# GpSimd's additions, subtractions and x's transposes moved behind another VectorE operation in a fused convolution and feed-forward kernel

## The chip, the cores and the metric

The kernel runs on one core of a Trainium2 chip. The metric is the device time of one execution in microseconds (us), the median over several runs. TensorE (PE in the profile; PEld is its weight load) does matrix products, VectorE (DVE), ScalarE (ACT) and GpSimd (POOL) do elementwise work, and SyncE (SP) issues most transfers. Each engine works through its own instructions in order.

## The reference

A light convolution over time (seven taps, one weight set for each of 8 heads) is followed by a feed-forward layer without gating, whose activation is a smooth step between -1 and 1:

```python
x_unf = x_pad[:, idx, :].reshape(B, S, K, H, group)      # B, S, D = 8, 4096, 192; K = 7, H = 8
x = np.einsum('hk,bskhg->bshg', softmax(weight), x_unf).reshape(B * S, D)
h = x @ w_in                                              # 192 x 2048
g = np.where(h >= 1, h, np.where(h <= -1, 0.0, (h + 1) ** 2 / 4))
return g @ w_out                                          # 2048 x 192
```

## The kernel before

**Tiles and steps.** The 32768 tokens are cut into 64 tiles of 512. A tile has 8 steps, one for each 256 of the 2048 hidden units, so there are 512 steps q. Tiles go in pairs c of 16 steps, called a period here; i is the step's number in its period, tile 2c has i from 0 to 7 and tile 2c+1 has i from 8 to 15. After the first 16 steps every product of 32-bit numbers is made of three products of a high half (rounded by ScalarE's copy to the matmul's 32-bit format) and a low half (what the rounding left, by a subtraction).

**One step** is written down in the main loop in this order: `mm1(q)` (18 matmuls on each half of the array, into one of two PSUM tiles `h`), `mm2(q - 3)`, `act_both(q)` (ScalarE: Relu and Square), on some steps `evac_banks` (four copies by ScalarE), `act_low(q - 2)` (VectorE: the low half of the activation, 128x1024, from two operands in SBUF), the slot of the convolution, `act_sum(q - 2)` (VectorE: the sum of two low halves), transfers and transposes of the output, `act_hi(q - 1)` (ScalarE) and `act_most(q)` (VectorE: reads `h` in PSUM and thereby frees it for `mm1(q + 2)`). `mm1` reads the tile's inputs in the order n, s, r: as they are, swapped between the partitions' halves, and the last 64 channels. In each of n and s it takes two matmul pairs on the high half and then one on the low half, so the swapped low half (`"s", "lo"`) comes with the second pair of low matmuls of the step.

**The convolution** for the tiles to come is spread over the steps in three units of a pair c: `a` is the first 128 channels of tile 2c, `b` those of tile 2c+1, `r` the last 64 channels of both. A unit is transposed by VectorE (`"T"`), gets its seven taps (0 to 6), and is split into a high and a low half, each of which is copied into a swapped version by two transfers on SP's queue (`swapped`). The plans say which step does what: `PLAN_A` and `PLAN_R` and the first part of `PLAN_B` (i of 12 and more) run in the period before the pair's own, the rest of `PLAN_B` (i under 8) in the pair's own first tile. `conv_slot` carries a plan out. Unit a's taps are VectorE's; a tap of b or r is a product on ScalarE (`product`) and an addition on GpSimd.

**Order of GpSimd's additions.** From c = 2 on, `taps` puts an addition into the list `held`. `add_held` issues the list behind the slot and makes each addition wait for that step's `act_sum`, so that it doesn't run beside `act_low`:

```python
add_held(act_sum(n) if low else None)
```

The subtraction that makes a low half in `split` for a and b is issued in the slot itself and waits for nothing but its operands. `evac_add` issues accumulating transfers on GpSimd's queue in the fourth and fifth step of each tile.

Of the kernel before, what the change touches and what calls it, by code (L numbers as in the profile page):

```python
# [8 lines left out]
F32 = mybir.dt.float32  # L9
# [22 lines left out]
def lightconv_then_ffn(ctx: ExitStack, tc: tile.TileContext, x, weight, w_in, w_out, out):  # L32
# [24 lines left out]
    nc = tc.nc  # L57
# [53 lines left out]
    def load_unit(c, u, engs=None):  # L111
        ta, tb = 2 * c * TB, (2 * c + 1) * TB
        if u == "rb":
            return load_raw([tb, tb, tb + TB // 2, tb + TB // 2], [P, P + SQ, P, P + SQ], engs,
                            TB // 2)
        if u == "r":
            return load_raw([ta, ta, tb, tb], [P, P + SQ, P, P + SQ], engs)
        return load_raw([ta if u == "a" else tb] * 4, [0, SQ, 2 * SQ, 3 * SQ], engs)
# [2 lines left out]

    pending = []

    held = []

    def add_held(behind):

        for out, a, b in held:
            add = nc.gpsimd.tensor_add(out, a, b)  # L129
            if behind is not None:  # L130
                tc.add_manual_dep(add.ins, behind.ins.name, mybir.DependencyInfo(
                    mybir.DependencyClass.Sync, mybir.DependencyReason.DATA), reason="port")
        held.clear()

    def let_go():

# [10 lines left out]
    class Conv:  # L147
# [92 lines left out]
        def taps(self, *ks):  # L240
            y = self.y
            for k in ks:
                if k == 0:
                    nc.scalar.mul(y, self.xT[:, SH:SH + TB], wk[:, self.wsel, 0:1])  # L244
                elif self.c == 1 and self.u != "b":
                    pending.append((y, y, self.product(k)))
                elif self.c > 1:
                    held.append((y, y, self.product(k)))
                else:
                    nc.gpsimd.tensor_add(y, y, self.product(k))  # L250

# [4 lines left out]
            nc.sync.dma_start(out=w[BOT].bitcast(F32), in_=t[TOP].bitcast(F32))  # L256
            return w

        def split(self, eng=None):
            for _ in self.splits(eng or nc.gpsimd):  # L260
                pass

        def splits(self, eng):

            o = xop[2 * self.c + (self.u == "b")]
            hi = xo.tile([P, TB], F32R, name="hi0")
            lo = xo.tile([P, TB], F32R, name="lo0")
            nc.scalar.copy(hi, self.y)
            for key, t in (("hi", hi), ("lo", lo)):
                if key == "lo":  # L270
                    yield
                    eng.tensor_sub(lo, self.y, hi.bitcast(F32))
                w = self.swapped(t, key + "1", 3)
                o["n", key] = (t[TOP], t[BOT])
                o["s", key] = (w[TOP], w[BOT])
            yield

        def split_rest(self):

# [157 lines left out]
    NQ = NSB * NPAIR  # L437
# [63 lines left out]
    turns = tc.alloc_semaphore("turns")  # L501
# [79 lines left out]
    def act_sum(q):  # L581
        gt = stage.tile([P, CC], F32R, name="m")[:, 0:TB]
        gts[q] = gt
        gl = gls[q].bitcast(F32)
        return nc.vector.tensor_add(gt, gl[:, 0, :], gl[:, 1, :])  # L585
# [214 lines left out]
    def whole(j, *cols):  # L800
        for _ in chunks[j].bits(*cols):
# [19 lines left out]
    conv_b, conv_rb = Conv(0, "b", raw_b), Conv(0, "rb", raw_rb)  # L821
# [5 lines left out]

    PLAN_B = {12: ("T",), 14: (0, 1), 15: (2, 3), 1: (4,), 2: (5,), 3: (6,), 5: "split"}  # L830
    PLAN_A = {1: ("T",), 2: (0,), 4: (1,), 6: (2,), 7: (3,), 9: (4,), 10: (5,), 11: (6,),
              12: "split"}
    PLAN_R = {2: ("T",), 4: (0,), 6: (1,), 7: (2,), 8: (3, 4), 9: (5,), 11: (6,), 13: "split"}
    SECOND_B = {0: (0, 1), 1: (2,), 2: (3,), 3: (4,), 4: (5, 6), 5: "split"}


# [2 lines left out]
    FIRST_A = {7: ("T", 0, 1, 2), 8: (3, 4), 9: (5, 6), 11: "split"}  # L839
    FIRST_R = {8: ("T",), 9: (0,), 10: (1, 2), 11: (3, 4), 12: (5, 6), 13: "split"}  # L840

    def conv_slot(i, b, a, r):
        early = b is not None and b.c == 0
        plans = ((None if early else b, SECOND_B if b and b.c == 1 else PLAN_B),
                 (a, FIRST_A if early else PLAN_A),
                 (r, FIRST_R if early else PLAN_R))
        for u, plan in plans:
            what = plan.get(i, ()) if u else ()
            if what == "split":
                if u is r:  # L850
                    u.split_rest()
                else:
                    u.split()
                continue
            if "T" in what:
                u.transpose()
            ks = [k for k in what if k != "T"]
            if ks:
                (u.taps_dve if u is a and not early else u.taps)(*ks)

# [5 lines left out]
    def parts_hi(q):  # L868
        for n, rest in PARTS.get(q, ()):
            chunks[n].hi(rest)  # L870
# [95 lines left out]
    conv_n, ahead = {}, {}  # L966
    for q in range(NQ + LATE):
        s, j = divmod(q, NPAIR)
        c, i = divmod(q, 2 * NPAIR)
        if q < NQ and i == 0 and c > 0:  # L970
            conv_b = conv_n["b"]
        if q < NQ and i == (0 if c > 0 else 4):
            conv_n, ahead = ahead, {}
            if c > 0 and c + 1 < NB:
                for u in "arb":
                    if u not in conv_n:
                        conv_n[u] = Conv(c + 1, u, load_unit(c + 1, u))
        if c == 0 and i in (4, 5, 10):
            u = {4: "a", 5: "r", 10: "b"}[i]
            conv_n[u] = Conv(1, u, load_unit(1, u))  # L980
        if i == (14 if c == 0 else 8) and c + 2 < NB:
            ahead = {u: Conv(c + 2, u, load_unit(c + 2, u)) for u in "ar"}

        done = q - (DELAY if q < NF32 + DELAY else LATE)
        if done < 0 or q == NF32 + DELAY:
            done = None
        if q == NPAIR:
            mm2_first(done)
        if q < NQ:
            mm1(q)  # L990
        if done is not None and q != NPAIR:
            (pair_last if done == NQ - 1 else mm2 if done >= NF32 else mm2_first)(done)

        if q < 2:
            (step_0, step_1)[q]()
        elif q < NPAIR:
            first_step(q)
        elif q < NF32:
            if q == NPAIR + 1:
                evac(0)  # L1000
            if q == 2 * NPAIR - 2:
                pending.extend(late)
            let_go()
            act_clip(q)
            act_square(q)
            parts_hi(q + 1)
            parts_lo(q, (True,))
            let_go()
            act_max(q)
            parts_lo(q, (False,))  # L1010
            conv_slot(i, conv_b, conv_n.get("a"), conv_n.get("r"))
            if j >= NPAIR - 2:
                store(0, "mr"[j - NPAIR + 2])
        else:
            if q == NQ - 1:
                act_hi(q - 1)
            if q < NQ:
                act_both(q)
            if done is not None and done % NPAIR == NPAIR - 1 and done < NQ - 1:
                (evac if done < NF32 else evac_banks)(done // NPAIR)  # L1020
            if done == NQ - 2:
                evac_last(done // NPAIR)
            if q == NF32:
                parts_lo(q)
            n = q - 1 if q < NF32 + 3 else q - 2
            low = n in ghs and n not in gls
            ahead_of = q in (NF32 + 2, NF32 + 3)
            if low:
                act_low(n)
            if ahead_of:  # L1030
                act_most(q)
            if q < NQ:
                conv_slot(i, conv_b if i < 8 else conv_n.get("b"), conv_n.get("a"),
                          conv_n.get("r"))
            add_held(act_sum(n) if low else None)
            if q == NQ - 1:
                act_low(q - 1)
                act_most(q)
                act_sum(q - 1)
            if q < NQ:  # L1040
                if s > 2 and j in (3, 4):
                    evac_add(s - 1, j - 3)
                if s <= 2 or s == NSB - 1:
                    m = 6 if s > 2 else 2
                    if m <= j < m + 2:
                        store(s - 1, "mr"[j - m])
                elif j == NPAIR - 1:
                    store(s - 1, "m")
                if j == 0 and s > 3:
                    store(s - 2, "r")  # L1050
            if q - 1 in gs and q - 1 not in ghs and q < NQ:
                act_hi(q - 1)
            if q < NQ - 1 and not ahead_of:
                act_most(q)
            if q < NF32 + 2:
                act_hi(q)
        if i == 2 * NPAIR - 1 and c == 0:
            conv_n["b"].transpose()
        if q == NQ - 4:
            plain = ob.tile([P, TB // SQ, SQ], F32, name="osb").rearrange("p j b -> p (j b)")[:, 0:P]  # L1060
            diagonal(plain, 0)
# [26 lines left out]
```

## Time and profile before

| | |
|---|---|
| median of 3 runs | 2046.57 us (2046.46 to 2049.79) |
| the profiled execution: time, span of its instructions | 2046.76 us, 2045.0 us |
| PE busy | 2037.9 us (100%) |
| PEld busy | 1756.9 us (86%) |
| DVE busy | 1966.2 us (96%) |
| ACT busy | 1960.4 us (96%) |
| POOL busy | 792.8 us (39%) |

Busy time is the union of an engine's instructions over the span. The ends of matmuls are modelled, and neighbours on an engine overlap a little, so a share near 100% doesn't tell whether an engine ever waits. The chain of work that ended last lies to 68% on PE, 15% on DVE and 13% on ACT. L579 is `act_low`, L585 `act_sum`, L890 `act_most`, L562 and L563 `act_both`, L573 `act_hi`, L475 `mm1`, L528 `mm2`, L129 the additions of `add_held`, L272 the subtraction of `splits`, L255 and L256 the swap copies, L163 the units' transposes, L631 the output's, L232 VectorE's taps, L237 ScalarE's products.

### The profile page before, as it was taken

To read this page: it belongs to the slowest core of one execution; us is meant where nothing else is said; L and a number is where in the kernel's file an instruction comes from. 1 tells how busy PE (TensorE), PEld (TensorE's weight loads), DVE (VectorE), ACT (ScalarE), POOL (GpSimd) and SP (SyncE) were. 2 spreads that over 40 slices of the span, in tenths; PEclk is the share of its full clock that TensorE was granted. 3 is DMA by queue.
4 is the path that set the end of the run, shared out by engine and by line. 5 is a ranking of instruction groups with operands and counts; after the bars stand their busy time and mean duration, and the time that the engine had idled before them with its cause. 6 is when DMAs were issued, how large, how long until landed. Compare 5 with 4: busy or idle time off the path is not lost.

```text
span 2045.0 us, 46902 instructions
## 1 busy us (share of the span) xinstructions
PE 2037.9 (100%) x18644; PEld 1756.9 (86%) x18644; DVE 1966.2 (96%) x2109; ACT 1960.4 (96%) x2381; POOL 792.8 (39%) x749
## 2 busy tenths in 40 slices
PE   9999999999999999999999999999999999999999
PEld 6998888888888888888888888888888888888888
DVE  8899999999999999999999999999999999999998
ACT  8799999999999999999999999999999999999997
POOL 1544343343433443334434344343343333443431
PEclk9999999999999999999999999999999999999999
DMA  7333333443434434334333344343343433433323
GB/s 178 80 62 70 69 71 71 85 76 56 81 68 79 80 65 77 71 67 87 70 66 73 72 82 76 57 83 69 74 81 65 76 71 66 86 72 65 72 55 55
DMA packets 470685, 152.27 MB, mean 74 GB/s; under 512 B 418944, under 2 KB 426624, under 8 KB 470464
## 3 DMA queue, kind: packets, MB, share of 16 engines
q1 hardware_dynamic: 446880, 109.17, 25.4%
q0 software_dynamic: 23424, 39.99, 13.4%
q8 instruction: 146, 2.39, 0.5%
q14 instruction: 75, 0.61, 0.1%
q10 hardware_dynamic: 160, 0.10, 0.0%
HBM read 32.84 MB, written 25.17 MB: 28 GB/s over the span
## 4 chain that ended last, share of the span: by engine, by line
PE 68%; DVE 15%; ACT 13%; issue 4%; DVEq 0%; ACTq 0%; POOL 0%; POOLq 0%
PE h L475 35%; PE accr L528 20%; PE accm L528 10%; DVE gl L579 7%; DVE g L890 4%; ACT gh L573 3%; ACT g L562 3%; ACT g L563 3%; DVE m L585 3%; ACT p L237 3%; DVE osb L631 1%; PE accm L495 1%; PE accr L495 1%; ACT t L609 0%; ACT y L244 0%
## 5 line engine op out<-in xcount | busy, mean ns | idle before, releaser
L579 DVE TENSOR_TENSOR gl<-g,gh 128x1024 fp32r<-128x1024 f32 x495 | 728.1, 1471 | 23.4 <-ACT gh L573 17.1
L890 DVE SCALAR_TENSOR_TENSOR g<-g,h 128x1024 f32<-128x1024 f32 x504 | 607.5, 1206 | 4.8 <-ACT g L563 2.8
L475 PE MATMUL h<-hi,w 64*128 64x512 f32 x4032 | 609.4, 380 | 1.5
L528 PE MATMUL accr<-gh,wg 64*128 64x512 f32 x3960 | 590.1, 376 | 0.0
L562 ACT ACTIVATE g<-h 128x1024 f32<-128x1024 f32 (+1 forms) x497 | 507.2, 1020 | 41.6 <-PE h L475 39.9
L563 ACT ACTIVATE g<-g 128x1024 f32<-128x1024 f32 (+1 forms) x497 | 526.6, 1060 | 15.8
L573 ACT CAST gh<-g 128x1024 fp32r<-128x1024 f32 x495 | 514.4, 1039 | 0.5 <-DVE g L890 0.4
L129 POOL TENSOR_TENSOR y<-y,p 128x512 f32<-128x512 f32 x180 | 231.0, 1283 | 573.3 <-ACT p L237 300.5
L475 PEld LDWEIGHTS h<-hi,w 64*128 64x128 f32 x4032 | 376.0, 186 | 76.4 <-DVE g L890 28.2
L528 PEld LDWEIGHTS accr<-gh,wg 64*128 64x128 f32 x3960 | 373.9, 185 | 53.2
L129 POOL TENSOR_TENSOR r<-r,p 128x512 f32<-128x512 f32 x180 | 232.5, 1291 | 476.6 <-DVE m L585 420.0
L475 PE MATMUL h<-lo,w 64*128 64x512 f32 x2016 | 383.8, 376 | 0.0
L528 PE MATMUL accr<-gl,words 64*128 64x512 f32 x1980 | 376.3, 376 | 0.0
L585 DVE TENSOR_TENSOR m<-gl 128x512 fp32r<-128x512 f32 x495 | 348.0, 703 | 20.6 <-PE h L475 0.5
L528 PE MATMUL accm<-gh,wg 64*128 64x512 f32 x1980 | 295.1, 376 | 0.0
L475 PE MATMUL h<-rh,w 64*128 64x512 f32 x992 | 293.6, 376 | 0.0
L475 PE MATMUL h<-rhi,w 64*128 64x512 f32 x992 | 293.6, 376 | 0.0
L619 POOL DMA_DIRECT2D t<-t x244 | 206.0, 983 | 97.6 <-DMA t<-t 75.6
L475 PEld LDWEIGHTS h<-lo,w 64*128 64x128 f32 x2016 | 192.2, 186 | 25.9
L528 PEld LDWEIGHTS accr<-gl,words 64*128 64x128 f32 x1980 | 188.3, 186 | 26.0
L528 PEld LDWEIGHTS accm<-gh,wg 64*128 64x128 f32 x1980 | 188.0, 186 | 26.0
L475 PEld LDWEIGHTS h<-rhi,w 64*128 64x128 f32 x992 | 184.5, 186 | 12.9
(161 smaller groups left out, 2313.3 us busy)
## 6 DMA issues: line engine op xcount, KB each, us to landing
t<-t POOLq DMA_DIRECT2D x183, 128.0 KB, 4.1
out_dram<-osb SPq DMA_DIRECT2D x366, 64.0 KB, 1.9
raw<-in_x_dram SPq DMA_DIRECT2D x334, 68.0 KB, 2.6
hi<-hi SPq DMA_DIRECT2D x128, 128.0 KB, 3.4
lo<-lo SPq DMA_DIRECT2D x126, 128.0 KB, 3.1
t<-t POOLq DMA_DIRECT2D x61, 256.0 KB, 3.3
rhi<-rh SPq DMA_DIRECT2D x62, 128.0 KB, 4.1
rlo<-rl SPq DMA_DIRECT2D x62, 128.0 KB, 3.5
```

The lines of the kernel that those rows point to most:

```text
L129: add = nc.gpsimd.tensor_add(out, a, b)
L237: nc.scalar.mul(p, self.xT[:, SH + k:SH + k + TB], wk[:, self.wsel, k:k + 1])
L475: nc.tensor.matmul(h[e], w[HALVES[e], c0:c0 + P], seen(x[e][e]), start=(n == 0), stop=(n == len(mms) - 1))
L495: nc.tensor.matmul(accs[s][a, i][:, c0:c0 + D], block, w[half, e, :], start=(j == 0 and e == 0 and b % 2 == 0), stop=(j == NPAIR - 1 and e ...
L528: mm = nc.tensor.matmul(accs[s][bank], w[half], in_turn(g[half]), start=(j == 0 and bank not in seen), stop=(j == NPAIR - 1 and k % 3 == 2 ...
L562: nc.scalar.activation(g[:, e, :], hs[q][:, e, :], AF.Relu, bias=0.5, scale=0.5)
L563: nc.scalar.activation(g[:, e, :], g[:, e, :], AF.Square)
L573: nc.scalar.copy(gh[:, e, :], gs[q][:, e, :])
L579: nc.vector.tensor_sub(gl[:, e, :], g[:, e, :], gh[:, e, :])
L585: return nc.vector.tensor_add(gt, gl[:, 0, :], gl[:, 1, :])
L619: nc.gpsimd.dma_start(out=to, in_=src, accum_op=ALU.add)
L890: nc.vector.scalar_tensor_tensor(out=g, in0=g, scalar=1.0, in1=h, op0=ALU.min, op1=ALU.max)
```

## The change

- `held` gets a second list, `fresh`. What a slot puts into `fresh` is issued by `add_held` one step later, behind that step's `act_sum`. The product on ScalarE is made in the slot as before.
- For a and b of c = 2 and more, the subtraction of the low half (and with it the two transfers of the swapped low half, which are written down behind it) goes into `fresh` as well. The high half and its transfers stay in the slot.
- `conv_slot` is called twice, once ahead of `act_sum` for what is not a transpose and once behind `add_held` for the entries with `"T"`.
- Taps 5 and 6 of r are done by VectorE (`taps_dve`).
- The plans of b, a and r are laid anew; the steps of the three splits stay.

```diff
 
     pending = []
-    held = []
+    held, fresh = [], []
     def add_held(behind):
-        for out, a, b in held:
-            add = nc.gpsimd.tensor_add(out, a, b)
+        for work in held:
+            done = work()
             if behind is not None:
-                tc.add_manual_dep(add.ins, behind.ins.name, mybir.DependencyInfo(
+                tc.add_manual_dep(done.ins, behind.ins.name, mybir.DependencyInfo(
                     mybir.DependencyClass.Sync, mybir.DependencyReason.DATA), reason="port")
-        held.clear()
+        held[:] = fresh
+        fresh.clear()
     def let_go():
...
                 elif self.c == 1 and self.u != "b":
                     pending.append((y, y, self.product(k)))
                 elif self.c > 1:
-                    held.append((y, y, self.product(k)))
+                    fresh.append(lambda p=self.product(k): nc.gpsimd.tensor_add(y, y, p))
                 else:
                     nc.gpsimd.tensor_add(y, y, self.product(k))
...
             nc.sync.dma_start(out=w[BOT].bitcast(F32), in_=t[TOP].bitcast(F32))
             return w
-        def split(self, eng=None):
-            for _ in self.splits(eng or nc.gpsimd):
-                pass
+        def split(self):
+
+            if self.c < 2:
+                for _ in self.splits(nc.gpsimd):
+                    pass
+                return
+            parts = self.splits(nc.gpsimd)
+            next(parts)
+            fresh.append(lambda: next(parts))
         def splits(self, eng):
...
             hi = xo.tile([P, TB], F32R, name="hi0")
             lo = xo.tile([P, TB], F32R, name="lo0")
             nc.scalar.copy(hi, self.y)
+            sub = None
             for key, t in (("hi", hi), ("lo", lo)):
                 if key == "lo":
                     yield
-                    eng.tensor_sub(lo, self.y, hi.bitcast(F32))
+                    sub = eng.tensor_sub(lo, self.y, hi.bitcast(F32))
                 w = self.swapped(t, key + "1", 3)
                 o["n", key] = (t[TOP], t[BOT])
                 o["s", key] = (w[TOP], w[BOT])
-            yield
+            yield sub
         def split_rest(self):
...
-    PLAN_B = {12: ("T",), 14: (0, 1), 15: (2, 3), 1: (4,), 2: (5,), 3: (6,), 5: "split"}
-    PLAN_A = {1: ("T",), 2: (0,), 4: (1,), 6: (2,), 7: (3,), 9: (4,), 10: (5,), 11: (6,),
+    PLAN_B = {13: ("T",), 14: (0, 1), 15: (2,), 0: (3,), 1: (4,), 2: (5,), 3: (6,), 5: "split"}
+    PLAN_A = {1: ("T",), 2: (0,), 4: (1,), 5: (2,), 6: (3,), 7: (4,), 9: (5,), 10: (6,),
               12: "split"}
-    PLAN_R = {2: ("T",), 4: (0,), 6: (1,), 7: (2,), 8: (3, 4), 9: (5,), 11: (6,), 13: "split"}
+    PLAN_R = {3: ("T",), 4: (0,), 6: (1,), 7: (2,), 8: (3,), 9: (4,), 11: (5,), 12: (6,),
+              13: "split"}
     SECOND_B = {0: (0, 1), 1: (2,), 2: (3,), 3: (4,), 4: (5, 6), 5: "split"}
...
     FIRST_A = {7: ("T", 0, 1, 2), 8: (3, 4), 9: (5, 6), 11: "split"}
     FIRST_R = {8: ("T",), 9: (0,), 10: (1, 2), 11: (3, 4), 12: (5, 6), 13: "split"}
-    def conv_slot(i, b, a, r):
+    def conv_slot(i, b, a, r, turns=None):
         early = b is not None and b.c == 0
         plans = ((None if early else b, SECOND_B if b and b.c == 1 else PLAN_B),
                  (a, FIRST_A if early else PLAN_A),
                  (r, FIRST_R if early else PLAN_R))
         for u, plan in plans:
             what = plan.get(i, ()) if u else ()
+            if turns is not None and turns != ("T" in what):
+                continue
             if what == "split":
                 if u is r:
                     u.split_rest()
...
                 u.transpose()
             ks = [k for k in what if k != "T"]
             if ks:
-                (u.taps_dve if u is a and not early else u.taps)(*ks)
+                dve = not early and (u is a or u is r and ks[0] > 4)
+                (u.taps_dve if dve else u.taps)(*ks)
...
             if ahead_of:
                 act_most(q)
             if q < NQ:
-                conv_slot(i, conv_b if i < 8 else conv_n.get("b"), conv_n.get("a"),
-                          conv_n.get("r"))
+                units = conv_b if i < 8 else conv_n.get("b"), conv_n.get("a"), conv_n.get("r")
+                conv_slot(i, *units, turns=False)
             add_held(act_sum(n) if low else None)
+            if q < NQ:
+                conv_slot(i, *units, turns=True)
             if q == NQ - 1:
                 act_low(q - 1)
                 act_most(q)
```

## Rows read from the trace of the kernel before

**Rows 1.** Busy times in windows, 146.65 to 1971.32: busy (instructions) of each engine.

```profile
146.65:1971.32 1824.67, 1821.91 (x16708) 1571.00 (x16705) 1773.50 (x1828) 1774.47 (x2118) 722.32 (x659) 1.00 0.39 73
```

**Rows 2.** Timeline, PE: start us, us, engine, line, operation, operands, count.

```profile
146.65 0.60 PE L475 MATMUL h<-hi,w 64*128 64x512 f32 x4
...
979.91 0.59 PE L475 MATMUL h<-hi,w 64*128 64x512 f32 x4
...
995.45 0.59 PE L475 MATMUL h<-hi,w 64*128 64x512 f32 x4
...
1971.32 0.59 PE L475 MATMUL h<-hi,w 64*128 64x512 f32 x4
```

**Rows 3.** Table of waits: who waited for whom, total us, times, longest us.

```profile
PEld h L475 <- DVE g L890: 28.2, 83, 0.5
```

**Rows 4.** Groups of instructions: busy us, mean ns, idle before and its releasers.

```profile
L579 DVE TENSOR_TENSOR gl<-g,gh 128x1024 fp32r<-128x1024 f32 x495 | 728.1, 1471 | 23.4 <-ACT gh L573 17.1
...
L237 ACT ACTIVATE p<-r,wk 128x512 f32<-128x512 f32 x180 | 124.1, 705 | 0.0
...
L232 DVE SCALAR_TENSOR_TENSOR y<-xT,wk,y 128x512 f32<-128x512 f32 x186 | 138.6, 745 | 0.1
...
L163 DVE STREAM_TRANSPOSE r<-raw 128x544 f32<-128x544 f32 x30 | 22.0, 732 | 0.0
```

**Rows 5.** Timeline, POOL and DVE, 965 to 967.5.

```profile
965.46 2.65 POOL L129 TENSOR_TENSOR y<-y,p 128x512 f32<-128x512 f32 x2 [2.33 <-ACT p L237]
...
966.91 2.28 DVE L579 TENSOR_TENSOR gl<-g,gh 128x1024 fp32r<-128x1024 f32 x1 [0.17 <-ACT gh L573]
```

**Rows 6.** Timeline, POOL and SP, around one split of b.

```profile
989.61 1.27 POOL L272 TENSOR_TENSOR lo<-y,hi 128x512 fp32r<-128x512 f32 x1 [0.56 <-ACT hi L268]
...
993.38 1.28 POOL L129 TENSOR_TENSOR r<-r,p 128x512 f32<-128x512 f32 x1 [2.49 <-DVE m L585]
...
991.05 1.22 SPq L255 DMA_DIRECT2D lo<-lo  x1
...
992.32 0.60 SPq L256 DMA_DIRECT2D lo<-lo  x1
```

**Rows 7.** Timeline, DVE, steps 3 to 7 of the same period.

```profile
979.92 1.53 DVE L579 TENSOR_TENSOR gl<-g,gh 128x1024 fp32r<-128x1024 f32 x1 [0.28 <-ACT gh L573]
...
983.49 1.53 DVE L579 TENSOR_TENSOR gl<-g,gh 128x1024 fp32r<-128x1024 f32 x1
...
987.34 1.21 DVE L579 TENSOR_TENSOR gl<-g,gh 128x1024 fp32r<-128x1024 f32 x1
...
990.50 1.46 DVE L579 TENSOR_TENSOR gl<-g,gh 128x1024 fp32r<-128x1024 f32 x1
...
992.55 0.68 DVE L585 TENSOR_TENSOR m<-gl 128x512 fp32r<-128x512 f32 x1
...
994.28 1.46 DVE L579 TENSOR_TENSOR gl<-g,gh 128x1024 fp32r<-128x1024 f32 x1
```

**Rows 8.** Timeline, DVE in step 13, and PE two steps later.

```profile
1019.94 0.69 DVE L283 TENSOR_TENSOR rl<-r,rh 128x512 fp32r<-128x512 f32 x1 [0.73 <-ACT rh L282]
1020.55 0.69 DVE L585 TENSOR_TENSOR m<-gl 128x512 fp32r<-128x512 f32 x1
1021.15 1.22 DVE L890 SCALAR_TENSOR_TENSOR g<-g,h 128x1024 f32<-128x1024 f32 x1
...
1022.66 0.60 PE L475 MATMUL h<-hi,w 64*128 64x512 f32 x4
```

**Rows 9.** Line 631 alone: duration min/median/max ns, first and last start, forms.

```profile
L631 DVE STREAM_TRANSPOSE osb<-t x122: 696/708/711, 147.8 to 2036.4; 128x512 f32<-128x512 f32 x61, 64x512 f32<-64x512 f32 x61
```

**Rows 10.** Timeline, PE: second pair of low matmuls in step 8.

```profile
996.53 0.38 PE L475 MATMUL h<-lo,w 64*128 64x512 f32 x2
```

**Rows 11.** Tile lo: its transfers on SP's queue (ns), and DMA to landing.

```profile
L255 SPq DMA_DIRECT2D lo<-lo x63: 461/500/1817, 45.8 to 1997.6; - x63
...
DMA to landing us min/median/max: 2.2/3.1/4.2
```

## What the change is expected to do

> **What bounds the kernel now.** I read the busy times of the steady stretch first [rows 1]: TensorE (1821.91 of 1824.67 us), VectorE (1773.50) and ScalarE (1774.47) are all nearly full, so shares decide nothing. The next question is what a step costs TensorE when nothing holds it, read from its timeline at the first matmul of a step. From the start of one period's step 4, 979.91, to that of its step 8, 995.45 [rows 2], it takes 15.54 / 4 = 3.885 us a step, or 62.16 a period of 16 steps. Over the 29 periods from 146.65 to 1971.32 [rows 2] a period takes 1824.67 / 29 = 62.92. So steady state holds only 0.76 us of waiting a period, some 23 us over the 30 periods that carry the planned work: that is all that the change can win there, whatever it frees on the other engines. The table of waits puts TensorE's loss at weight loads that wait for `act_most` (28.2 us, [rows 3]; a load waits a little earlier than its matmul, so this is the larger figure). The clock was granted in full all the way [rows 1] and plays no part.
>
> Behind `act_most` stands VectorE. `act_low` takes 1.47 us on average [rows 4]. It grows when a GpSimd add runs into it; the worst case is two adds in a row at the end of a period (2.65 us from 965.46), which stretch the next `act_low` to 2.28 [rows 5].
>
> **The change part by part.**
>
> **Adds a step behind.** The product is there a step early, so GpSimd can start right behind `act_sum`, as it does now in step 6, where it waited for nothing else: the sum starts at 992.55 and ends some 0.68 later, the add starts at 993.38, 0.15 after that, and takes 1.28 [rows 6, 7]. `act_most`, which reads one operand from PSUM and follows the sum, covers most of it; what sticks out costs the next `act_low` 0.25 (1.46 at 994.28 against 1.21 at 987.34, [rows 7]). With one add a step the 1.07 of the double add goes (2.28 less 1.21), and so does 0.32 each at 979.92 and 983.49 [rows 7], where the add came late behind its product.
>
> **Transposes behind the sum.** A transpose of 0.73 [rows 4] delays its follower by some 0.66, as neighbours on VectorE overlap by about 0.07 (1019.94 + 0.69 against 1020.55, [rows 8]). Three of them go between sum and `act_most`. The output's transposes stand there already, beside a running add, and keep 0.70 to 0.71 in all 122 cases [rows 9], so I cost the move at no contention, and the transpose completes the add's cover. The price is that `act_most` of that step comes 0.66 later. In steps 1 and 3 VectorE has room. In step 13 it has not: there the low half of r has waited 0.73 for ScalarE's copy, `act_most` ends at 1021.15 + 1.22 = 1022.37, and TensorE takes the freed bank at 1022.66 [rows 8]. B's transpose moves into this step: 1022.37 + 0.66 = 1023.03, 0.37 late. If ScalarE, a product lighter at step 11, reaches r's copy earlier, it is as little as nothing. I take 0.15 a period, nearer to the lower end, since that copy waits for ScalarE alone.
>
> **Two taps to VectorE.** ScalarE loses two products of 0.7, VectorE gains two operations of 0.74 [rows 4], 0.66 in a row. Of VectorE's busy time 1.47 - 1.21 = 0.26 of each `act_low` is blocking, 4.2 a period, of which five cases of 0.25 to 0.28 remain (the adds of steps without a transpose): its demand changes by 1.3 + 1.4 - 4.2 = -1.5. Neither engine becomes the bound in total. By these three parts alone the 0.76 goes, except for the 0.15 of step 13.
>
> **The low halves a step behind.** This part decides, I think. The plan keeps B's split at step 5, and tile 2c+1 starts at step 8 as before. Now GpSimd computes the low half as soon as the high half exists, from 989.61 to 990.88, ahead of step 6's sum, and SP's queue issues the two swap copies at 991.05 and 992.32 [rows 6]. A copy lands 3.1 us after its issue (2.2 to 4.2, [rows 11]), here at 995.4. TensorE begins step 8 at 995.45 [rows 2] and reads the swapped low half in the step's second pair of low matmuls, at 996.53 [rows 10]. The margin is 1.1 us.
>
> Afterwards the subtraction waits for step 6's `act_sum`: it stands where r's add of that step stands, 993.38 to 994.66 [rows 6]. The second copy is issued some 0.6 later (the first holds the queue 0.50, [rows 11]) and lands, at the median, at 994.66 + 0.6 + 3.1 = 998.36, which is 1.83 behind 996.53. VectorE also comes to that sum later. Between step 3's `act_low` and step 6's sum, the late adds take 0.32 twice less, r's transpose comes in with 0.66, an add now stands behind step 4's sum (0.25), A's tap now falls into step 5 (at most 0.66, some 0.5 with the pause that a sum directly behind `act_low` has now), and step 6 loses its own 0.25: +0.5 in all, some 0.1 less since the start of the period is no longer late. That makes 2.2. Against it, the copies now run behind the high halves' copies and the accumulating transfers and no longer among them, so for the landing I take 2.9, below the median of all: **2.0 us a period**. Bounds: 0.9 with the shortest landing and VectorE where it is now, 3.4 with the longest and VectorE 0.5 later. TensorE works in order, so nothing covers the wait; `mm2`'s matmuls stand behind it. Behind the waiting subtraction GpSimd has the next add alone, and behind the copies SP has output stores and loads, which nobody waits for yet.
>
> A's subtraction moves from step 12 to step 13, but its tile starts only at step 16. The sum of step 13 ends at 1020.55 + 0.69 = 1021.24 [rows 8]; with 0.15, 1.28, 0.6 and 2.9 the copy lands at 1026.2. Step 16 starts a step behind 1022.66, at 1026.5, and reads it 1.08 later (as 996.53 less 995.45): 1.4 us in hand, and 0.1 with the longest landing.
>
> The Trainium skill ("SBUF — State Buffer", section "The DMA setup-cost knee") gives a transfer a fixed part of some 2 us plus its bytes at 436 GB/s, for these 128 KB an estimate of 2.3 us. The rows show 3.1 at the median, and they decide; by the page's figure the wait would be 1.4 and the time about 2071.
>
> **The sum.** The profiled execution took 2046.76 us (span 2045.0), 0.2 above the median of the runs. A period changes by +2.0 (swapped low half) + 0.15 (step 13) - 0.76 (the waits of now) = +1.39. B's split stands behind the sum in 30 periods (c from 2 to 31): +41.7, so 2046.8 + 41.7 = **2088.5 us**.
>
> **The rivals.**
> - *Short landing.* Without other transfers beside them the copies land near their shortest, 2.2: the wait is about 1.2 and the time 2046.8 + 30 x (1.2 + 0.15 - 0.76) = 2064.5. For it: now they share the queues with much. Against: 3.1 is the median over all copies, A's too. Chance 0.12. The page named above leans this way.
> - *The swap comes in time, and only the gains count* (faster). The place is step 8's second low pair. It decides if both copies land within 1.3 us of the subtraction's end, with the 0.6 for issuing in it; the shortest landing seen is 2.2 from issue. Or the subtraction isn't held as I read the diff. Then 2046.8 + 30 x (0.15 - 0.76) = 2028.5. Chance 0.05.
> - *VectorE late on top.* The taps and the transposes ahead of `act_most` make step 13 late by the full 0.37, the low half comes at 2.2, and A's swap is late by up to 0.5 too: 2046.8 + 30 x (2.2 + 0.37 + 0.5 - 0.76) = 2116. For it: VectorE hardly idles now. Against: a wait of 2 us at step 8 gives VectorE and ScalarE that much free time in each period. Chance 0.08.
> - My forecast, 2075 to 2105: 0.73. The last 0.02 is a wait so small (near 0.6) that loss and gains cancel.
>
> **How the numbers follow.** About 0.2% is what a measurement of this kernel can tell from no change, here 2042.5 to 2050.7. Even the lower bound of the wait, 0.9, gives 2055.5, so only the second rival is faster, and only the last case and a little more is the same: faster 0.05, same 0.03, slower 0.92. For 8 in 10 the range takes the forecast, most of the short landing and the lower part of the third rival: 2062 to 2114.
>
> **What would show it.** Right: in each period of the trace after, step 8's low matmuls wait about 2 us for the transfer that writes `lo`, and hardly any load waits for `act_most`; B's subtraction stands just behind step 6's sum; `act_low` is near 1.3 on average and never 2.28; the transposes keep 0.73. A wait in step 15 for step 13's `act_most` is the 0.15. Wrong: steps of 3.885 throughout the period (the copies come in time), an `act_low` as long as now (the adds are still late), or TensorE idle at other steps.

## The result and the profile after

The changed kernel takes 2070.41 us (2069.62 to 2070.85), the kernel before beside it 2046.82: a ratio of 1.0113, with an interval of 1.0098 to 1.0128. It is slower by 1.1%, as forecast and inside the range, but the step is little more than half of the one expected (23.6 us for 41.7).

The page's engine table and the shares of the chain that ended last, of the changed kernel (2070.61 us in the profiled execution, span 2068.9):

```profile
PE 2049.7 (99%) x18644; PEld 1842.7 (89%) x18644; DVE 1882.3 (91%) x2169; ACT 1932.4 (93%) x2321; POOL 709.7 (34%) x689
...
PE 52%; DVE 20%; ACT 13%; issue 6%; DMA 5%; POOL 2%; SPq 1%; DVEq 0%; ACTq 0%; POOLq 0%
```

VectorE and ScalarE have become emptier (96% before, both) while the kernel became slower: what holds TensorE now is not work. The chain names it: 5% of it are transfers (3% the copies of `lo`), which the chain of before did not have.

TensorE's timeline in a period of the changed kernel, first matmul of a period at the ends and step 8 in the middle ([rows 2, 10] before; L483 is `mm1`):

```profile
147.58 0.59 PE L483 MATMUL h<-hi,w 64*128 64x512 f32 x4
...
1007.04 0.59 PE L483 MATMUL h<-hi,w 64*128 64x512 f32 x4
1007.47 0.38 PE L483 MATMUL h<-lo,w 64*128 64x512 f32 x2
1007.69 0.59 PE L483 MATMUL h<-hi,w 64*128 64x512 f32 x4
1008.65 1.11 PE L483 MATMUL h<-lo,w 64*128 64x512 f32 x2 [0.37 <-DMA lo<-lo]
...
1012.08 0.70 PE L483 MATMUL h<-hi,w 64*128 64x512 f32 x4
...
1995.47 0.59 PE L483 MATMUL h<-hi,w 64*128 64x512 f32 x4
```

A period takes (1995.47 - 147.58) / 29 = 63.72 us, against 62.92. Step 8 lasts from 1007.04 to 1012.08, 5.04 us in place of 3.885, so 1.15 are lost there; in the other periods of the stretch it lasts 5.00 to 5.07. The second pair of low matmuls should start 1.08 behind the step (1008.12). Its first half starts at 1008.65, and its second only at 1009.28 (1.11 us for two matmuls of 0.38 to 0.48 each that otherwise stand side by side); what ended the wait is the transfer that writes `lo`. The sum, the subtraction and the two copies ahead of it, from the timelines of DVE, POOL and SP ([rows 6, 7] before):

```profile
1004.28 0.68 DVE L593 TENSOR_TENSOR m<-gl 128x512 fp32r<-128x512 f32 x1
...
1005.10 1.28 POOL L280 TENSOR_TENSOR lo<-y,hi 128x512 fp32r<-128x512 f32 x1 [4.42 <-ACT p L238]
...
1006.41 0.46 SPq L256 DMA_DIRECT2D lo<-lo  x1
...
1006.91 0.60 SPq L257 DMA_DIRECT2D lo<-lo  x1
```

GpSimd starts 0.14 behind the sum's end (1004.28 + 0.68) and is done at 1006.38; the copies are issued at 1006.41 and 1006.91, the second lands just ahead of 1009.28, 2.4 later. The view of the tile gives a landing of 2.2 at the median of all copies of low halves, where it was 3.1 [rows 11]:

```profile
DMA to landing us min/median/max: 2.1/2.2/4.2
```

The table of waits (total us, times, longest) and two groups of instructions (busy us, mean ns, idle before) of the changed kernel, for [rows 3, 4]:

```profile
DVE gl L587 <- ACT gh L581: 111.0, 68, 2.3
...
PEld h L483 <- DMA lo<-lo: 35.1, 58, 0.8
...
PEld h L483 <- DVE g L902: 17.8, 61, 0.5
...
PE h L483 <- DMA lo<-lo: 12.7, 43, 0.4
```

```profile
L587 DVE TENSOR_TENSOR gl<-g,gh 128x1024 fp32r<-128x1024 f32 x495 | 619.7, 1252 | 113.9 <-ACT gh L581 111.0
...
L164 DVE STREAM_TRANSPOSE r<-raw 128x544 f32<-128x544 f32 x30 | 22.1, 737 | 0.0
```

`act_low` fell from 1471 to 1252 ns, near the 1.21 us of one with no addition beside it [rows 7], and VectorE now waits 111.0 us for ScalarE where it waited 17.1 [rows 4]: most of the contention that the change goes after is gone, and the time saved is idle time. Loads waiting for `act_most` fell from 28.2 to 17.8 us, and 35.1 us of waiting for `lo` have come in.

Most of the rest of the loss comes from step 13 and shows in the two steps behind it ([rows 8] before; DVE, then POOL, then TensorE at the starts of steps 14, 15 and 16):

```profile
1032.52 0.69 DVE L291 TENSOR_TENSOR rl<-r,rh 128x512 fp32r<-128x512 f32 x1 [1.00 <-ACT rh L290]
1033.13 0.68 DVE L593 TENSOR_TENSOR m<-gl 128x512 fp32r<-128x512 f32 x1
1033.73 0.74 DVE L164 STREAM_TRANSPOSE xT<-raw 128x544 f32<-128x544 f32 x1
1034.39 1.18 DVE L902 SCALAR_TENSOR_TENSOR g<-g,h 128x1024 f32<-128x1024 f32 x1
...
1033.95 1.28 POOL L280 TENSOR_TENSOR lo<-y,hi 128x512 fp32r<-128x512 f32 x1 [6.22 <-ACT gh L581]
...
1031.51 0.70 PE L483 MATMUL h<-hi,w 64*128 64x512 f32 x4
...
1035.63 0.70 PE L483 MATMUL h<-hi,w 64*128 64x512 f32 x4
...
1039.62 0.59 PE L483 MATMUL h<-hi,w 64*128 64x512 f32 x4
```

The low half of r waits 1.00 us for ScalarE's copy, then come the sum, b's transpose and, from 1034.39, `act_most`, which ends at 1035.57. Step 15 should have started at 1031.51 + 3.885 = 1035.39 and starts at 1035.63, 0.24 late; step 15 itself then lasts 3.99, another 0.10. The transpose ran beside GpSimd's subtraction and took its 0.74 all the same.

A last, small loss stands in step 5 (DVE in step 3, then TensorE at the starts of steps 5 and 6):

```profile
991.45 1.22 DVE L587 TENSOR_TENSOR gl<-g,gh 128x1024 fp32r<-128x1024 f32 x1 [2.01 <-ACT gh L581]
...
995.32 0.66 PE L483 MATMUL h<-hi,w 64*128 64x512 f32 x4
...
999.27 0.59 PE L483 MATMUL h<-hi,w 64*128 64x512 f32 x4
```

Step 5 lasts 3.95, so 0.07 too long. The steps other than these four (5, 8, 14 and 15) last 3.885.

### The profile page after: what moved, and what is told of

It reads as the page before. It is cut to its first block, busy times and chain, and to the rows that moved or that the text cites. A ratio compares the mean times of both kernels' runs of the same rounds, so it can differ in the third digit from the quotient of the medians.

```text
span 2068.9 us, 46749 instructions
## 1 busy us (share of the span) xinstructions
PE 2049.7 (99%) x18644; PEld 1842.7 (89%) x18644; DVE 1882.3 (91%) x2169; ACT 1932.4 (93%) x2321; POOL 709.7 (34%) x689
## 4 chain that ended last, share of the span: by engine, by line
PE 52%; DVE 20%; ACT 13%; issue 6%; DMA 5%; POOL 2%; SPq 1%; DVEq 0%; ACTq 0%; POOLq 0%
PE h L483 26%; PE accr L536 15%; DVE gl L587 9%; PE accm L536 8%; DVE g L902 6%; DMA lo<-lo 3%; ACT gh L581 3%; ACT g L570 3%; ACT t L617 3%; DVE m L593 2%; ACT p L238 2%; POOL lo L280 2%; ACT g L571 1%; DVE r L164 1%; ACT hi L275 1%
## 5 line engine op out<-in xcount | busy, mean ns | idle before, releaser
L587 DVE TENSOR_TENSOR gl<-g,gh 128x1024 fp32r<-128x1024 f32 x495 | 619.7, 1252 | 113.9 <-ACT gh L581 111.0
L536 PE MATMUL accr<-gh,wg 64*128 64x512 f32 x3960 | 638.2, 377 | 0.0
L483 PE MATMUL h<-hi,w 64*128 64x512 f32 x4032 | 634.8, 379 | 0.1
L483 PEld LDWEIGHTS h<-hi,w 64*128 64x128 f32 x4032 | 423.6, 186 | 48.3 <-DVE g L902 17.8
L483 PE MATMUL h<-lo,w 64*128 64x512 f32 x2016 | 436.7, 379 | 14.8 <-DMA lo<-lo 12.7
L536 PEld LDWEIGHTS accr<-gh,wg 64*128 64x128 f32 x3960 | 407.3, 185 | 39.1
L536 PE MATMUL accr<-gl,words 64*128 64x512 f32 x1980 | 421.4, 376 | 0.0
L483 PE MATMUL h<-rhi,w 64*128 64x512 f32 x992 | 296.6, 379 | 0.0
L483 PE MATMUL h<-rh,w 64*128 64x512 f32 x992 | 293.6, 376 | 0.0
L483 PEld LDWEIGHTS h<-lo,w 64*128 64x128 f32 x2016 | 233.4, 186 | 51.2 <-DMA lo<-lo 35.1
L249 POOL TENSOR_TENSOR r<-r,p 128x512 f32<-128x512 f32 x120 | 154.1, 1284 | 315.3 <-DVE m L593 257.9
L536 PEld LDWEIGHTS accr<-gl,words 64*128 64x128 f32 x1980 | 232.6, 186 | 16.2
L536 PE MATMUL accm<-m,words 64*128 64x512 f32 x990 | 212.3, 376 | 0.0
```

The lines of the kernel that those rows point to most:

```text
L249: fresh.append(lambda p=self.product(k): nc.gpsimd.tensor_add(y, y, p))
L483: nc.tensor.matmul(h[e], w[HALVES[e], c0:c0 + P], seen(x[e][e]), start=(n == 0), stop=(n == len(mms) - 1))
L536: mm = nc.tensor.matmul(accs[s][bank], w[half], in_turn(g[half]), start=(j == 0 and bank not in seen), stop=(j == NPAIR - 1 and k % 3 == 2 ...
L587: nc.vector.tensor_sub(gl[:, e, :], g[:, e, :], gh[:, e, :])
```

## Experiments

All are compared with the changed kernel's 2070.4 us; ratios are to the kernel before, beside which they ran (2047.31 us beside the first four experiments, 2045.87 beside the others). Step 8's wait is written as its length less 3.885.

**b's low half at once.**

```diff
-            if self.c < 2:
+            if self.c < 2 or self.u == "b":
```

> The changed kernel, with b's low half subtracted in step 5's slot again, waiting for its operands alone; a's stays a step behind. Theory (b's swapped low half lands late): the excess of step 8, 1.15 us in each of 30 periods, goes to 0 and the rest stays (0.24 + 0.10 in steps 14 and 15, 0.07 in step 5): 2070.4 - 34.5 = 2036. Rival (the loss is VectorE's, from two more taps and transposes ahead of act_most): the wait comes back at act_most and the time stays within 3 us of 2070.

2034.82 us, ratio 0.9941 (0.9929 to 0.9953). TensorE's timeline, step 8, its second low pair and step 9, and the wait for `act_most` that is left:

```profile
991.80 0.60 PE L483 MATMUL h<-hi,w 64*128 64x512 f32 x4
...
992.88 0.38 PE L483 MATMUL h<-lo,w 64*128 64x512 f32 x2
...
995.69 0.60 PE L483 MATMUL h<-hi,w 64*128 64x512 f32 x4
```

```profile
PEld h L483 <- DVE g L902: 19.2, 66, 0.5
```

Step 8 lasts 3.89, its second low pair stands at its place, and the wait did not move to `act_most` (19.2 us against 17.8). This one line turns the change from 1.1% slower to 0.6% faster. The theory stands, and the rival, VectorE's lateness, falls. One part of the theory does not hold: the excess of step 14 did not stay at 0.24 but is 0.14 here (from 1015.11 to 1019.14). In the changed kernel the two halves of the array run 0.11 apart from step 8's wait to the end of step 14, and ScalarE begins on step 13's result 2.25 behind the step's start (1029.87 and 1027.62); here the halves run together, and it begins 2.15 behind (1013.38 and 1011.23).

**b's transpose a step earlier.**

```diff
-    PLAN_B = {13: ("T",), 14: (0, 1), ...
+    PLAN_B = {12: ("T",), 14: (0, 1), ...
```

> The changed kernel, with b's transpose behind the sum of step 12 and not of step 13. Theory (in step 13 act_most comes late by the transpose, since that step's chain through r's copy has no room): the 0.24 + 0.10 us of steps 14 and 15 go, step 8 keeps its 1.15: 2070.4 - 10 = 2060. Rival (a wait at step 8 covers what stands elsewhere in the period): no change, 2070.

2062.94 us, ratio 1.0078 (1.0065 to 1.009). The starts of steps 4, 5, 6, and of 14 and 15:

```profile
987.50 0.70 PE L483 MATMUL h<-hi,w 64*128 64x512 f32 x4
...
991.45 0.70 PE L483 MATMUL h<-hi,w 64*128 64x512 f32 x4
...
995.44 0.60 PE L483 MATMUL h<-hi,w 64*128 64x512 f32 x4
...
1027.68 0.70 PE L483 MATMUL h<-hi,w 64*128 64x512 f32 x4
...
1031.56 0.70 PE L483 MATMUL h<-hi,w 64*128 64x512 f32 x4
```

Step 14 is back at 3.88 and the kernel 7.5 us faster, so step 13's lateness was real and not covered by step 8's wait: the two add up, nearly (step 14's excess is 0.24 beside step 8's wait and 0.14 without it). It is less than the 10 expected, because steps 4 and 5 now take 3.95 and 3.99, a delay of 0.17 in place of 0.07. It starts where step 3's `act_most` is due, which has r's transpose ahead of it.

**r's channels ahead of the swapped halves.**

```diff
-            mms = [(W[j][:, part], u + u, [xop[s][u, x]] * 2) for u in "nsr"
+            mms = [(W[j][:, part], u + u, [xop[s][u, x]] * 2) for u in "nrs"
```

> The changed kernel, with mm1 reading the last 64 channels ahead of the swapped halves, so that the swapped low half is read three matmul pairs, 0.65 us, later in each step. Theory (TensorE waits at exactly that matmul for the second copy): step 8's 1.15 falls to 0.50, 2070.4 - 19.5 = 2051. Rival (TensorE is held at the start of the step, or by the PSUM banks): 2070.

2051.66 us, ratio 1.0023 (1.0013 to 1.0032). Step 8 of this kernel, its second low pair, and the start of step 9:

```profile
998.29 0.59 PE L483 MATMUL h<-hi,w 64*128 64x512 f32 x4
...
1000.01 0.99 PE L483 MATMUL h<-lo,w 64*128 64x512 f32 x2
...
1002.68 0.70 PE L483 MATMUL h<-hi,w 64*128 64x512 f32 x4
```

The pair is due 1.72 behind the step's start (1000.01) and its halves again come one after the other; the step lasts 4.39, so the wait fell from 1.15 to 0.50, by the 0.65 that its reader moved. TensorE is held at this matmul and at nothing in front of it.

**r's two taps back on ScalarE and GpSimd.**

```diff
-    PLAN_R = {3: ("T",), ... 9: (4,), 11: (5,), 12: (6,), ...
+    PLAN_R = {3: ("T",), ... 9: (4,), 10: (5,), 11: (6,), ...
...
-                dve = not early and (u is a or u is r and ks[0] > 4)
+                dve = not early and u is a
```

> The changed kernel, with r's taps 5 and 6 as products on ScalarE and additions on GpSimd again (steps 10 and 11, added a step later). Theory (the two taps are no load on VectorE that counts, and on ScalarE they make step 13's copy of r late): step 8 keeps its 1.15, ScalarE reaches step 13 some 0.9 us later, so the wait for act_most there grows from 0.24 to about 1.1: 2070.4 + 27 = 2097. Rival (the taps on VectorE are part of the loss): below 2070.

2096.67 us, ratio 1.0241 (1.0227 to 1.0255). The start of step 14 on PE, step 13 on DVE and the start of step 15, in the timeline, and the wait for `act_most` in the table of waits:

```profile
1043.75 0.70 PE L483 MATMUL h<-hi,w 64*128 64x512 f32 x4
...
1045.65 0.69 DVE L291 TENSOR_TENSOR rl<-r,rh 128x512 fp32r<-128x512 f32 x1 [1.30 <-ACT rh L290]
...
1047.52 1.18 DVE L902 SCALAR_TENSOR_TENSOR g<-g,h 128x1024 f32<-128x1024 f32 x1
...
1048.76 0.70 PE L483 MATMUL h<-hi,w 64*128 64x512 f32 x4 [0.63 <-DVE g L902]
```

```profile
PEld h L483 <- DVE g L902: 37.7, 61, 1.0
```

The copy of r is now waited for 1.30, `act_most` ends at 1048.70, and step 14 lasts 1048.76 - 1043.75 = 5.01, a wait of 1.12. ScalarE has no pause ahead of r's copy in this kernel and starts it 1.26 behind the start of step 14 (1045.01); in the changed kernel it waited 0.24 for `mm1` in step 13 and started the copy 0.38 behind (1031.89). (The two products also stand a step earlier than the taps did.) Having the two taps on VectorE, which looks like load on a full engine, is thus worth 26 us in this plan, because it lets ScalarE come to r's copy earlier.

**b's low half on VectorE, and both transposes elsewhere.**

```diff
-            parts = self.splits(nc.gpsimd)
+            parts = self.splits(nc.vector if self.u == "b" else nc.gpsimd)
...
+                self.parts = parts
...
+            if what == "low":
+                if u.c > 1:
+                    next(u.parts)
+                continue
...
-    PLAN_B = {13: ("T",), 14: (0, 1), ... 5: "split"}
+    PLAN_B = {12: ("T",), 14: (0, 1), ... 5: "split", 6: "low"}
-    PLAN_R = {3: ("T",), ...
+    PLAN_R = {2: ("T",), ...
```

> The changed kernel, with b's low half subtracted by VectorE in step 6's slot, b's transpose behind the sum of step 12 and r's behind that of step 2. Theory: the subtraction then ends about 1.4 us earlier than behind the sum on GpSimd, which is more than the 1.15 that the swapped low half is late, step 13's and step 3's act_most have room again, and VectorE has the 0.66 us to spare: no excess in any step, 2025. Rival (VectorE is full): act_most late somewhere, over 2035.

2025.54 us, ratio 0.9899 (0.9886 to 0.9913), as expected. The subtraction ends 2.79 ahead of step 8 (983.70 and 986.49), 2.1 earlier than the 0.66 of the changed kernel and not only 1.4, and the second copy lands at 986.59, 0.98 ahead of its read. In steady state all steps last 3.885, but for 0.01 more in step 9 and 0.03 in step 10.

**Three places undone.** The edit of the first experiment, the transposes of b at 12 and of r at 2.

> The changed kernel with three places undone: b's low half subtracted at once in step 5, b's transpose behind the sum of step 12, r's behind that of step 2. Theory (step 8's 1.15, steps 14 and 15 with 0.24 + 0.10, and step 5 with 0.07 have these three causes and no other): 2070.4 - 30 x 1.56 = 2024, every step at 3.885. Rival (GpSimd's subtraction beside act_low makes VectorE late): 2030 to 2035.

2024.53 us, ratio 0.9894 (0.9881 to 0.9908): the fastest version. TensorE's timeline, the first matmul of a period at both ends of 29 periods:

```profile
146.84 0.59 PE L483 MATMUL h<-hi,w 64*128 64x512 f32 x4
...
1949.48 0.60 PE L483 MATMUL h<-hi,w 64*128 64x512 f32 x4
```

That is (1949.48 - 146.84) / 29 = 62.16 us a period: every wait of steady state is gone, so step 8, step 13 and r's transpose in step 3 are all of the loss. This shows r's transpose by what is left over: the first two were undone alone above, and its move is the only other edit here.

**One part alone on the kernel before.** Only b's subtraction is put a step behind, where `add_held` issues it ahead of the step's additions.

```diff
+    lows, fresh = [], []
...
+        for work in lows:
+            done = work()
...
+            if self.c > 1 and self.u == "b":
+                next(parts)
+                fresh.append(lambda: next(parts))
+                return
...
```

> The kernel before with one part alone: b's low half is subtracted a step later, behind the sum of step 6 (ahead of r's addition there). Theory: the subtraction ends 0.1 us earlier than in the changed kernel, so step 8 waits 1.0 us in 30 periods, and of the 0.76 us of other waits those behind step 8 (about 0.4) go: 2046.8 + 30 x 0.6 = 2065, 2062 to 2078. Rival (it takes the whole change to make it slower): 2047.

2060.4 us, ratio 1.007 (1.0056 to 1.0083). Step 8, its second low pair and step 9 (L490 is `mm1` here):

```profile
1002.01 0.59 PE L490 MATMUL h<-hi,w 64*128 64x512 f32 x4
...
1003.25 1.10 PE L490 MATMUL h<-lo,w 64*128 64x512 f32 x2
...
1006.67 0.70 PE L490 MATMUL h<-hi,w 64*128 64x512 f32 x4
```

Step 8 lasts 4.66, a wait of 0.78 where 1.0 was expected: step 6's `act_low` has no subtraction beside it any more and takes 1.23 (at 997.06) where it took 1.46 (at 990.50 in [rows 7]), so the sum begins 3.15 ahead of step 8 (998.86) and not 2.90 as before, which the expectation left out. The part alone costs 14 us; the rival, that it takes the whole change, falls.

**Additions in the same step again**, on top of the three places undone.

```diff
-                    fresh.append(lambda p=self.product(k): nc.gpsimd.tensor_add(y, y, p))
+                    held.append(lambda p=self.product(k): nc.gpsimd.tensor_add(y, y, p))
```

> As e6_three_undone, and the additions of GpSimd issued behind the sum of the same step again, as before the change; b's and a's plans stay laid anew, a's low half a step behind. Theory (most of the gain is that no step has two additions and that ScalarE has two products less; a product that comes late costs the next act_low 0.3, for which there is room): 2024 to 2030. Rival (the step behind is what frees act_low): 2035 or more.

2025.86 us, ratio 0.9901 (0.9888 to 0.9915). `act_low` in the groups of instructions, first with the additions a step behind (three places undone), then with them in the same step:

```profile
L587 DVE TENSOR_TENSOR gl<-g,gh 128x1024 fp32r<-128x1024 f32 x495 | 625.9, 1264 | 78.0 <-ACT gh L581 78.0
```

```profile
L587 DVE TENSOR_TENSOR gl<-g,gh 128x1024 fp32r<-128x1024 f32 x495 | 657.7, 1329 | 52.0 <-ACT gh L581 48.6
```

The step behind shortens `act_low` by 65 ns, and the kernel by 1.3 us of 21. The rest comes from the other parts together, the new plans, the place of the transposes, the taps and a's low half; they were not taken apart further. The theory's reason, one addition a step and two products less on ScalarE, is therefore not shown to be the one.

## Why the prediction was right, and what it sized wrongly

**The bound.** That steady state had only 0.76 us a period to give, whatever was freed, held to the end: the fastest version stands at 62.16.

**The step that decides.** The subtraction of b's low half stood just behind step 6's sum, its copies were late for step 8's second low pair, and TensorE waited in each of 30 periods, as forecast. The term was 2.0 us and measured 1.15. Two parts of it were too large. From the subtraction's end to the read it took 1009.28 - 1006.38 = 2.90, where 0.6 + 2.9 = 3.5 was put in: the landing was taken near the median of the rows of before [rows 11], which was made among other transfers. A copy of the same 128 KB took 2.2 at the median in the changed kernel, and 2.7 with b's subtraction at once, in its old place. Taken by unit the difference is plainer. In steady state b's two copies landed 3.2 and 2.7 after their issue in the kernel before (medians), 2.2 and 2.3 with b's low half alone a step behind on that kernel, 2.2 and 2.3 in the changed kernel, and 3.3 and 3.0 there with b's low half at once. So the later place makes the landing shorter, in either kernel. That it is the neighbours in the queues that make the difference was argued and not tried. And VectorE came to the sum only 0.14 later (2.76 ahead of step 8's start, 1004.28 and 1007.04, against 2.90 before, 992.55 and 995.45) where 0.4 was put in: the sum of single durations counted time as work in which VectorE waited for ScalarE. In the kernel before, step 4's `act_low` began at 983.49 [rows 7] only when ScalarE's copy was done (983.45; VectorE was free at 983.38), so part of r's transpose fell into a pause.

The sum with the measured sizes: 1.15 + 0.34 + 0.07 - 0.76 = +0.80 a period, 24 us in 30 periods; 23.6 were measured.

The measured 2070.4 lies between the rival of the short landing (2064.5) and the forecast's own band, 2075 to 2105: the mechanism and the place were right, and the band that had most of the chance was missed. The shortest landing of before, 2.2 [rows 11], was the row to take. By the forecast's own terms it makes the wait 2.0 - (2.9 - 2.2) = 1.3 and the time 2067.5; the rival put 1.2. The Trainium skill ("SBUF — State Buffer", "The DMA setup-cost knee") agrees with the trace here: its estimate of 2.3 us for the copy stands against 2.2 at the median and 2.4 from the second copy's issue to its reader. The section's 436 GB/s is its limit over 16 ports; whether copies between 64 partitions come near that rate no run here shows. That the time worked out from it, about 2071, is within 1 us of the measured one is partly luck: the sum's lateness was 0.26 too large in it (0.4 for 0.14), and steps 13 and 3 were 0.26 too small (0.15 for 0.34 + 0.07).

**Step 13.** The place was right, the size was not: 0.15 was taken between 0 and 0.37, and it cost 0.24 and 0.10 in the step behind. The reason given for the low value, that ScalarE would be there earlier, reaches only so far: in the changed kernel ScalarE's step 13 begins at 1029.87 after 0.24 of waiting for `mm1`'s result, and cannot begin earlier. Part of the 0.24 that step 14 loses comes from step 8's wait, without which it is 0.14, near the size forecast; the 0.10 in step 15 was not in the sum.

**Step 3.** "VectorE has room" was wrong in step 3: r's transpose ahead of its `act_most` costs 0.07 to 0.17 a period. The row that told it stood in [rows 7]: step 3's `act_low` had waited 0.28 for ScalarE, which makes four more copies in step 2, so that step begins late on VectorE whatever else is freed. In the changed kernel the same `act_low` waits 2.01.

**What was to show it.** `act_low` was forecast near 1.3 on average and never 2.28; it is 1.25, and 1.68 at the longest of 495. **What was costed at nothing** held: transposes beside a running addition took 737 ns (732 before), the two taps cost VectorE nothing that counts, and a's low half, a step later as well, came in time. One sign failed: hardly any load was to wait for `act_most`, and loads still waited 17.8 us for it, behind steps 13 and 3.

## What to carry to other kernels

An operation that is put off so as not to disturb another takes with it all that is written down behind it, transfers included; follow it to its last reader and compare the whole way (queue, duration, issue, landing) with the time until that read, not until the step. When three engines are nearly full, ask first what the one that sets the end has left to lose: here 0.76 us a period, so that 1.15 at one place outweighed all that was freed. A landing time read from a trace belongs to the moment in which it was read; for the copies that moved here, the shortest row was a better guide than the median.

## What the runs showed of the hardware

Two copies of 128 KB, issued 0.50 us apart on one queue, land 0.63 apart (1008.61 and 1009.24), so that of two matmuls that run side by side on the array's halves the first starts at 1008.65 and the second 0.63 later; the wait of the pair is that of the later copy. A wait for a freed bank at the start of a step (0.24) was followed by 0.10 more in the next step, in the changed kernel, and likewise in the kernel before (steps from 967.93 to 972.04 and on to 976.03: 4.11 and 3.99). The trace shows where the 0.10 lies: behind such a wait the second pair of matmuls starts 0.32 behind the first, where it is 0.22 elsewhere, and the loads of the first pair start with their matmuls (1035.63) and not some 0.2 ahead. It is the same 0.10 behind waits of 0.14 (b's low half at once), 0.24 and 1.12 (r's two taps back). In step 5 the loads wait too little to hold the first pair, and the second comes 0.28 behind it: that is its 0.07. What makes the gap was not tried.

The wait for a transfer in the middle of step 8 does something else: step 9 is back at 3.885, and the two halves of the array, which start 0.00 to 0.01 apart in step 7, stay 0.11 apart until the wait for a bank at the start of step 15 brings them together again.
